# Copying V straight from its PSUM banks to the head layout, and moving the tail turns, in a recurrent-memory attention kernel

## The chip, the cores and the metric

The kernel runs on one core of one Trainium2 chip, in one launch. The metric is the device time of that core in microseconds (us), from the first to the last instruction. Most executions of one kernel agree within 0.3%, so a difference of a few us needs several rounds on the same chip.

## The reference, cut to what matters

The program computes a transformer block with a memory-augmented, recurrent attention and a gated feed-forward part, and the gradients of all weights and inputs. The change concerns the forward pass of the attention alone. There the sequence of 2048 rows is cut into 64 segments of 32 rows; each segment attends to itself and to 8 memory rows, and the first 8 rows of its result are the memory of the next. So segments can't run at the same time: the end of one is the beginning of the next.

```python
B, S, Dm = (1, 2048, 512); H, Dh = (32, 128); M, seg = (8, 32)
for s in range(n_seg):                               # 64 segments, one after the other
    xs = x[:, s * seg_len:(s + 1) * seg_len, :]
    h = jnp.concatenate([mem, xs], axis=1)           # 40 rows
    q = jnp.einsum('btd,dhe->bhte', h, Wq)
    k = jnp.einsum('btd,dhe->bhte', h, Wk)
    v = jnp.einsum('btd,dhe->bhte', h, Wv)
    scores = jnp.where(mask, jnp.einsum('bhqe,bhke->bhqk', q, k) * scale, -1e9)
    p = _softmax(scores, axis=-1)
    o = jnp.einsum('bhqk,bhke->bhqe', p, v)
    o = jnp.einsum('bhte,hed->btd', o, Wo)
    mem = o[:, :M, :]                                # the next segment's memory
    outs.append(o[:, M:, :])
```

## The kernel before

**The layouts.** A projection multiplies the 32 first rows of a segment (the memory and 24 rows of its own) by all 32 heads. TensorE does it in 128x32 tiles, so one PSUM bank of 128 partitions holds four groups of heads, 32 rows each, side by side in the partitions. Groups 0 to 2 already lie where attention wants them: the head layout packs three heads into 96 partitions. Group 3 (partitions 96 to 127) holds the last eight heads, the "far" ones, and these must move to partitions 0 to 95. The last 8 rows of each segment (the "tail" rows) don't depend on the memory; they are projected four segments at a time, ahead of need, and brought in separately.

**One segment** runs in this order. `proj` projects one half of the heads and copies the bank to rows in SBUF (`RA`). `turns` transposes the K and Q rows on TensorE; each turned bank is then copied by ScalarE or VectorE, first the "own" heads, then the far ones.

```python
def turn_half(self, psp, rows, hf):                  # one tile (one bank) per tensor and half
    tp = psp.tile([128, 4, 128], BF16, name="turn_ps", tag="p")
    for i in range(4):
        self.nc.tensor.transpose(tp[:, i, :], rows[...], self.ident[:, :])
    return tp
...
proj("k", 0, "dve"); proj("k", 1, "act")             # line breaks joined
proj("q", 0, "dve"); proj("q", 1, "act")
proj("v", 0, "dve")
nc.gpsimd.tensor_copy(Vst[0:96, 0:512], RA["v"][0:96, 0:512])
turns()
proj("v", 1, "dve")
nc.gpsimd.tensor_copy(Vst[0:96, 512:1024], RA["v"][0:96, 512:1024])
...
st_exp(0)                                            # scores on TensorE, exponential on ScalarE
st_exp(1)
vshift()                                             # the moving product
st_exp(2)
```

V needs no transpose, only its far heads moved. That is `vshift`: three TensorE products with an identity block carry partitions 96 to 127 of the V rows to partitions 0 to 95 of a PSUM bank, and VectorE copies the bank to `Vst`.

```python
def vshift():
    sh = ps_f32("sh_ps")
    shf = sh[:].rearrange("p g x -> p (g x)")
    for hl in range(3):
        nc.tensor.matmul(shf[32 * hl:32 * hl + 32, 0:384], lhsT=self.ident[96:128, 96:128],
                         rhs=RA["v"][96:128, 384 * hl:384 * hl + 384], start=True, stop=True,
                         tile_position=(96, 32 * hl))
    nc.vector.tensor_copy(Vst[0:96, 1024:1408], shf[0:96, 0:384])
```

Then come, in three parts of 4, 4 and 3 groups of heads, the denominators (`den`, products with ones), PV (`pv`), the reciprocals, the scaled results `Ost`, their turns (`ott`) and the output projection. The denominators of all groups lie in the last column block of one bank, `or2`, whose first three blocks later take the third part of PV.

```python
or2 = ps_f32("or_ps")
den(0, or2); or0 = pv(0); ...
den(1, or2); or1 = pv(1)
recip(0, 2, or2)                                     # VectorE reads or2[:, 3, 0:8]
ost(0, or0, "dve")
ost(1, or1, "act")                                   # four scalings
pv(2, or2)                                           # TensorE writes or2[:, 0:3, :]
den(2, or2); recip(2, 3, or2); ost(2, or2, "dve")
...
fill(s4, "turn")                                     # tail turns: s4 = s % 4 of 2 and 3
if s4 == 3:
    p1(s // nseg_t + P1_AHEAD, 4)                    # the turns of a later tile's layer norm
    turned = True
if more and not turned:
    mask_mm(more.pop(0))                             # the next segment's mask, put into a score bank
    mask_mm(more.pop(0))
ott(0)
... # a mask between the turns that follow, where one is left
ott(1); ott(2)
at_ps = outproj()
```

The program order of each engine is kept by dependencies that the kernel adds itself. All tiles with `tag="p"` share five PSUM buffers of one bank each; the scores have three of their own.

Of the kernel before, what the change touches and what calls it, by code (L numbers as in the profile page):

```python
# [7 lines left out]
BF16 = mybir.dt.bfloat16  # L8
# [32 lines left out]
class K:  # L41
# [392 lines left out]
    def phase2(self):  # L434
        nc, tc, cfg, io = self.nc, self.tc, self.cfg, self.io
        D, DC, H, E, L, M, T, G, NS = cfg.D, cfg.DC, cfg.H, cfg.E, cfg.L, cfg.M, cfg.T, cfg.G, cfg.NS
        GW = 128
        NP = 3
# [9 lines left out]
        with ExitStack() as ctx:  # L448
# [10 lines left out]
            def ps_f32(name):  # L459
                return psp.tile([128, PG, GW], F32, name=name, tag="p")  # L460
# [4 lines left out]
            def ptiles(name, n, zero=True, w=G * GW):  # L465
                ts = []
                for i in range(n):
                    t = pt.tile([128, w], BF16, name=f"{name}{i}")
                    if zero:
                        zeros.append(lambda t=t, w=w: nc.vector.memset(t[:, 1024:w] if w == 9 * 128 else t[:], 0.0))  # L470
                    ts.append(t)
                return ts
# [6 lines left out]
            Vsts = ptiles("Vst", 2)  # L479
            Ost = ptiles("Ost", 1)[0]  # L480
            OT = ptiles("OT", 1)[0]
            RAs = [{x: ptiles(f"RA{i}" + x, 1, w=9 * 128)[0] for x in ("vkq", "kq")[i]} for i in range(2)]
            RAs[1]["v"] = RAs[0]["v"]
            RB = {x: ptiles("RB" + x, 1, w=9 * 128)[0] for x in "kq"}
            RBv = ptiles("RBv", 2, w=9 * 128)

# [1 line left out]
            P1_AHEAD = 2  # L488
# [64 lines left out]
            def part3(t, pi):  # L553
                return t[:, pi * PW:min((pi + 1) * PW, G * GW)].rearrange("p (g x) -> p g x", x=GW)
# [7 lines left out]
            Ws = {"q": Wq, "k": Wk, "v": Wv}  # L562

            def pass_half(x, hf, lhs, rows, eng):
                self.col_pass(psp, Ws[x], hf, lhs, rows, eng)

            def turn_half(rows, hf):
                return self.turn_half(psp, rows, hf)

            def to_heads(eng, xt, src, i0, n, w, o, own=True, far=True):  # L570


                b = 0 if w == 32 else 96
                s4 = src.rearrange("p i (j r) -> p i j r", r=32)
                if own:
                    d = xt[:, 120 * i0:120 * (i0 + n)].rearrange("p (i x) -> p i x", x=120)[:, :, b:b + 3 * w]
                    self.evac(eng, d.rearrange("p i (j r) -> p i j r", r=w), s4[:, :, 0:3, o:o + w])
                if not far:
                    return
                for a0, n0, hl in ((0, 3, 0), (3, 3, 1), (6, 2, 2)):  # L580
                    lo, hi = max(a0, i0), min(a0 + n0, i0 + n)
                    if lo < hi:
                        d = xt[:, 960:1320].rearrange("p (i r) -> p i r", r=120)[:, lo - a0:hi - a0]
                        self.evac(eng, d[:, :, b + w * hl:b + w * hl + w], s4[:, lo - i0:hi - i0, 3, o:o + w])

            def rows_out(rows, dram, s0, ns):

                if ns == 1:
                    nc.sync.dma_start(dram[s0, 0:96, 0:8, :].rearrange("r g e -> r (g e)"), rows[0:96, 0:1024])
                    nc.sync.dma_start(dram[s0, 0:96, 8:11, :].rearrange("(hl r) g e -> r hl (g e)", r=32),  # L590
                                      rows[96:128, :].rearrange("r (hl x) -> r hl x", hl=3))
                    return
                for j in range(3):
                    nc.sync.dma_start(dram[s0:s0 + 4, 96 + 8 * j:104 + 8 * j, 0:8, :].rearrange("s q g e -> s q (g e)"),
                                      rows[32 * j:32 * j + 32, 0:1024])
                for hl in range(3):
                    nc.sync.dma_start(dram[s0:s0 + 4, 96 + 8 * hl:104 + 8 * hl, 8:11, :].rearrange("s q g e -> s q (g e)"),
                                      rows[96:128, 384 * hl:384 * hl + 384])
# [44 lines left out]
            def fill(s4, where):  # L643
                for f in slots.pop((s4, where), []):
                    f()
# [35 lines left out]
            for s in range(NS):  # L681
# [9 lines left out]

                def proj(x, hf, eng):
                    pass_half(x, hf, lambda c: hT[:, c, :], RA[x], eng)
                    if hf == 1 and x != "v" and s < NS - 1:
                        rows_out(RA[x], DR[x], s, 1)

                def late_rows():
                    for x in "kq":
                        rows_out(RA[x], DR[x], s, 1)

                def turns():
                    tps = []
                    for x in "kq":
                        for hf in range(2):
                            tps.append((x, hf, ("act", "dve")[hf], turn_half(RA[x], hf)))
                            to_heads(tps[-1][2], XT[x], tps[-1][3][:], 4 * hf, 4, 32, 0, far=False)
                    for x, hf, eng, tp in tps:
                        to_heads(eng, XT[x], tp[:], 4 * hf, 4, 32, 0, own=False)

                def st_exp(pi):  # L710
                    st_ps = masked.pop(pi)
# [21 lines left out]
                        nc.tensor.transpose(ps[:, j, :], src[:, g * w:g * w + GW], self.ident[:, :])  # L733
                    return ps[:, 0:n, :], n

                def vshift():
                    sh = ps_f32("sh_ps")
                    shf = sh[:].rearrange("p g x -> p (g x)")
                    for hl in range(3):
                        nc.tensor.matmul(shf[32 * hl:32 * hl + 32, 0:384], lhsT=self.ident[96:128, 96:128],  # L740
                                         rhs=RA["v"][96:128, 384 * hl:384 * hl + 384], start=True, stop=True,
                                         tile_position=(96, 32 * hl))
                    nc.vector.tensor_copy(Vst[0:96, 1024:1408], shf[0:96, 0:384])

                def pv(pi, or_ps=None):
                    or_ps = or_ps or ps_f32("or_ps")
                    n = min(PG, G - pi * PG)
# [6 lines left out]
                def ost(pi, or_ps, eng):  # L754
                    n = min(PG, G - pi * PG)
                    if eng == "act":
                        for j in range(n):
                            g = pi * PG + j
                            nc.scalar.activation(Ost[0:120, g * GW:(g + 1) * GW], or_ps[0:120, j, :], AF.Copy,
                                                 scale=rden[:, g:g + 1])  # L760
                        return
                    nc.vector.tensor_tensor(part3(Ost, pi)[0:120, 0:n, :], or_ps[0:120, 0:n, :],
                                            rden[:, pi * PG:pi * PG + n].unsqueeze(2).to_broadcast([120, n, 128]), op=ALU.mult)

                def ott(pi):
                    ps, n = transposes_part(Ost, pi)
                    self.evac("dve" if pi == 1 else "act", part3(OT, pi)[:, 0:n, :], ps)

                def outproj():
                    ps = psp.tile([128, 256], F32, name="at_ps", tag="p")  # L770
# [18 lines left out]
                if s == 0:  # L789
                    for f in firsts["q"]:  # L790
                        f()
                    tails_in("kq", 0)
                proj("v", 0, "dve")
                nc.gpsimd.tensor_copy(Vst[0:96, 0:512], RA["v"][0:96, 0:512])
                turns()
                proj("v", 1, "dve")
                nc.gpsimd.tensor_copy(Vst[0:96, 512:1024], RA["v"][0:96, 512:1024])
                if s == 0:
                    for f in firsts["v"]:
                        f()  # L800
# [7 lines left out]
                    late_rows()  # L808
                st_exp(0)
                st_exp(1)  # L810
                vshift()
                st_exp(2)
                if s < NS - 1:
                    nc.sync.dma_start(VTr[:], Vst[:, :], transpose=True)
                or2 = ps_f32("or_ps")
                den(0, or2)
                or0 = pv(0)
# [8 lines left out]
                recip(0, 2, or2)  # L826
                ost(0, or0, "dve")
                ost(1, or1, "act")
                pv(2, or2)
                den(2, or2)  # L830
                recip(2, 3, or2)
                ost(2, or2, "dve")
                more = list(range(NP)) if s + 1 < NS else []
                turned = bool(slots.get((s4, "turn"))) or bool(mod_r)
                mod_row = mod_r.pop()() if mod_r else None
                if s + 1 in mod_at:
                    load, products = self.mod_rest(psp, sb2, mod_at.index(s + 1))
                    load()
                    mod_r.append(products)
                fill(s4, "turn")  # L840
                if s4 == 3:
                    p1(s // nseg_t + P1_AHEAD, 4)
                    turned = True
                if more and not turned:
                    mask_mm(more.pop(0))
                    mask_mm(more.pop(0))
                ott(0)
                if len(more) > 1:
                    mask_mm(more.pop(0))
                ott(1)  # L850
                if len(more) > 1:
                    mask_mm(more.pop(0))
                ott(2)
                if more:
                    mask_mm(more.pop(0))
                self.pop_later()
                self.pop_later()
                nc.sync.dma_start(self.OSR[s], gl3(Ost))
# [1279 lines left out]
```

The softmax here doesn't subtract the row's maximum and nothing guards it: scores larger than these inputs give would overflow.

## Time and profile before

| | |
|---|---|
| median of 3 runs | 3096.84 us (3094.25 to 3099.61) |
| span of the profiled run | 3093.9 us |
| TensorE clock granted, mean | 0.991 of full |
| first K turn of the first and of the last segment | 46.7 and 985.2 us |
| one cycle of four segments, 601.00 to 660.52 us | 59.52 us |
| mean DMA rate over the span | 227 GB/s |

The 64 segments of the forward attention fill the time from about 47 to about 1000 us, a third of the span. The rest (layer norms, feed-forward part, all gradients) isn't touched by the change. The views read here are the page with the busy share of each engine, the windows view (busy time of each engine in given stretches), the timeline (instructions in order of time, equal neighbours merged into one line), the chain of waits inside a window, and the answers for one tile or one line, which also tell what an engine waited for. In these, PE is TensorE's products, PEld its weight loads, DVE VectorE, ACT ScalarE and POOL GpSimd; the name of a tile stands without its buffer number. A product on PE is shown with its modelled length, pipelining included, so its start is the safer reading.

### The profile page before, as it was taken

Reading aid. Unit: us, or ns where it says so; the run is one execution under the profiler, and the core shown is the slowest. Engines: PE = TensorE matmul, PEld = TensorE weight load, DVE = VectorE, ACT = ScalarE, POOL = GpSimd, SP = SyncE. Lnnn points to the kernel's source line nnn. Section 1 sums busy time; section 2 is a strip of 40 time slices with the busy share of each in tenths; the row PEclk is TensorE's granted clock in tenths of the full one; section 3 lists DMA queues with packets and bytes.
Section 4 is the critical chain, followed back from the end, with each engine's and each line's share of the span. In section 5 each row is a group of like instructions: output and inputs, shape, how many; then the busy total and the mean of one; then the engine's idle time right before and its main releaser. Section 6 shows DMA issues by size and latency. Waiting matters only on the chain.

```text
span 3093.9 us, 106049 instructions
## 1 busy us (share of the span) xinstructions
PE 2997.4 (97%) x43769; PEld 1835.7 (59%) x43845; DVE 1628.3 (53%) x3799; ACT 1269.5 (41%) x3056; POOL 1378.6 (45%) x2958
## 2 busy tenths in 40 slices
PE   5999999999999899989999999999999999999999
PEld 3666666666665444445577777777777754445454
DVE  4556656665555788742255555555555642322221
ACT  2555555555555433322255555555555530111011
POOL 3666766666766222211244444444444422333322
PEclk8999999999999899999999999999999999999999
DMA  9887788788788799997599999999999998666574
GB/s 299 217 213 203 205 206 216 201 213 211 206 201 255 200 231 232 224 284 247 170 239 243 245 243 244 239 248 244 244 240 245 245 271 279 195 201 220 190 237 148
DMA packets 845944, 703.54 MB, mean 227 GB/s; under 512 B 544306, under 2 KB 717906, under 8 KB 845076
## 3 DMA queue, kind: packets, MB, share of 16 engines
q1 hardware_dynamic: 714148, 486.69, 62.3%
q0 software_dynamic: 60656, 148.64, 14.9%
q10 hardware_dynamic: 70656, 61.41, 6.4%
q8 instruction: 345, 5.65, 0.8%
q14 instruction: 139, 1.14, 0.1%
HBM read 294.93 MB, written 276.35 MB: 185 GB/s over the span
## 4 chain that ended last, share of the span: by engine, by line
PE 90%; DMA 4%; DVE 3%; issue 1%; POOL 1%; ACT 1%; SPq 0%; another core or an unknown queue 0%; DVEq 0%; POOLq 0%; ACTq 0%
PE pass_ps L255 18%; PE gps L1928 13%; PE dh_ps L215 8%; PE g_ps L1590 6%; PE gps5o L1942 4%; PE at_ps L223 4%; PE dhq_ps L223 4%; PE gps L1277 3%; PE mm L1121 3%; PE dh_tps L215 3%; PE turn_ps L264 2%; PE dp_ps L1569 2%; PE tps L1502 2%; PE tps L733 2%; PE mm L1081 2%; DVE RA0v L63 1%
## 5 line engine op out<-in xcount | busy, mean ns | idle before, releaser
L1928 PE MATMUL gps<-rows,hrows 128*128 128x512 bf16 (+2 forms) x2124 | 415.6, 355 | 1.9
L1928 PEld LDWEIGHTS <-hrows 128*128 128x128 bf16 x2160 | 211.2, 98 | 204.6
L255 PEld LDWEIGHTS <-hT 128*32 128x32 bf16 x6144 | 158.2, 97 | 161.3 <-issue 1.9
L1634 POOL COPY dOst<-RAd 96x512 bf16<-96x512 bf16 x128 | 75.4, 612 | 312.2 <-DVE RAd L63 312.2
L63 DVE CAST ot<-gps 128x512 bf16<-128x512 f32 (+3 forms) x76 | 48.1, 633 | 274.8 <-PE gps L1928 185.8
L1932 POOL DMA_DIRECT2D out_dram<-ot x108 | 81.3, 753 | 248.9 <-DVE ot L63 136.5
L61 ACT ACTIVATE ot<-gps 128x512 bf16<-128x512 f32 (+3 forms) x75 | 41.3, 551 | 349.5 <-PE gps L1928 221.7
L885 POOL TENSOR_TENSOR Pst<-Pst,rden 120x1408 bf16<-120x1408 bf16 x63 | 159.6, 2533 | 43.8 <-issue 28.4
L61 ACT ACTIVATE dVT<-g_ps 128x512 bf16<-128x512 f32 (+1 forms) x192 | 109.5, 570 | 95.3 <-PE g_ps L1590 95.0
L63 DVE CAST RA0v<-pass_ps 128x512 bf16<-128x512 f32 x128 | 88.5, 692 | 89.4 <-PE pass_ps L255 85.5
L215 PE MATMUL dh_ps<-WvT,dVT 128*32 128x512 bf16 x2048 | 133.4, 380 | 0.2 <-DVE RBd L63 0.2
L255 PE MATMUL pass_ps<-Wv,hT 128*32 128x512 bf16 x2048 | 133.3, 380 | 0.0
L1942 PE MATMUL gps5o<-WoT,rows 128*128 128x512 bf16 x580 | 127.8, 379 | 3.9 <-DMA rows<-OSR 3.2
L255 PE MATMUL pass_ps<-Wk,hT 128*32 128x512 bf16 x2048 | 123.3, 383 | 1.5 <-ACT hT L875 1.1
L1579 DVE SCALAR_TENSOR_TENSOR dS<-dp_ps,Pst_l 128x512 bf16<-128x512 f32 (+1 forms) x192 | 112.1, 640 | 22.1 <-PE dp_ps L1577 22.1
L223 PE MATMUL at_ps<-Wo,OT 128*32 128x256 bf16 x4096 | 123.5, 273 | 0.1
L255 PE MATMUL pass_ps<-WoT,dyT 128*32 128x256 bf16 (+1 forms) x3072 | 122.4, 308 | 0.9 <-ACT dyT L1708 0.9
L223 PE MATMUL dhq_ps<-WqT,dQT 128*32 128x256 bf16 x4096 | 122.9, 273 | 0.0
L215 PE MATMUL dh_ps<-WkT,dKT 128*32 128x512 bf16 x2048 | 122.2, 380 | 0.0
L255 PE MATMUL pass_ps<-Wq,hT 128*32 128x512 bf16 x2048 | 121.6, 379 | 0.0
L223 PEld LDWEIGHTS <-dQT 128*32 128x32 bf16 x4096 | 109.6, 97 | 15.9
L717 ACT ACTIVATE ET<-st_ps 128x480 bf16<-128x480 f32 (+1 forms) x192 | 96.0, 535 | 42.6 <-ACT qT L61 34.7
(419 smaller groups left out, 7082.2 us busy)
## 6 DMA issues: line engine op xcount, KB each, us to landing
OSR<-Ost SPq DMA_DIRECT2D x64, 352.0 KB
OT<-OT SPq DMA_DIRECT2D x64, 352.0 KB
VT<-VTr SPq DMA_DIRECT2D x64, 352.0 KB
PS<-Pst SPq DMA_DIRECT2D x64, 352.0 KB
OT_l<-OT SPq DMA_DIRECT2D x64, 352.0 KB
Pst_l<-PS SPq DMA_DIRECT2D x64, 352.0 KB
VT_l<-VT SPq DMA_DIRECT2D x64, 352.0 KB
DVR<-rows_x POOLq DMA_DIRECT2D x64, 352.0 KB, 6.4
```

Source lines behind the costliest of these rows:

```text
L61: return nc.scalar.activation(out, in_, AF.Copy)
L63: return nc.vector.tensor_copy(out, in_)
L215: self.nc.tensor.matmul(ps[32 * j:32 * j + 32, :], lhsT=lhsT, rhs=w, start=(n < 4), stop=(n >= total - 4), tile_position=(0, 32 * j))
L223: nc.tensor.matmul(ps[32 * j:32 * j + 32, :], lhsT=x[k], rhs=w[k][:, 256 * d:256 * d + 256], start=(n == 0), stop=(n == total - 1), tile_p ...
L255: self.nc.tensor.matmul(ps[32 * j:32 * j + 32, :], lhsT=lhs(c), rhs=rhs, start=(c == 0), stop=(c == DC - 1), tile_position=(0, 32 * j))
L717: nc.scalar.activation(part3(ET, pi)[:, 0:n, 0:120], st_ps[:, 0:n, 0:120], AF.Exp, scale=cfg.scale)
L885: nc.gpsimd.tensor_tensor(Pst[0:120, :, :], Pst[0:120, :, :], rden[:, :].unsqueeze(2).to_broadcast([120, G, 128]), op=ALU.mult)
L1121: nc.tensor.matmul(hp[:], lhsT=xT[:, fc, :], rhs=wT[:, fc, :], start=(n == 0), stop=(n == 2 * FC - 1))
L1579: nc.vector.scalar_tensor_tensor(out=part3(dS, pi), in0=ps[:, 0:n, :], scalar=cfg.scale, in1=part3(Pst, pi), op0=ALU.mult, op1=ALU.mult)
L1590: nc.tensor.matmul(ps[:, j, :], lhsT=lh[:, g * GW:(g + 1) * GW], rhs=rh[:, g * GW:(g + 1) * GW], start=True, stop=True)
L1928: nc.tensor.matmul(ps[:, 0:ng * E], lhsT=hrows[:, tp_, c * 128:(c + 1) * 128], rhs=rows[:, tp_, 0:ng * E], start=(tp_ == 0), stop=(tp_ == ...
L1942: nc.tensor.matmul(pss[gg][:], lhsT=src[0][:, src[1], gg * E:(gg + 1) * E], rhs=dyrows[:, tp_, :], start=(tp_ == order[0]), stop=(tp_ == o ...
```

## The change

V goes from its two banks straight to `Vst`: VectorE copies the own heads of each half, and the far heads are copied across partitions by ScalarE (first half) and VectorE (second half). The moving products, the V rows in SBUF and GpSimd's two copies of them are gone. The V banks now stay in use until the far copies have read them; the turns of K and Q, which took four tiles, take two, so that K's and Q's turns of one half share a tile. Tail turns, modulation products and (where s mod 4 = 3) the layer norm's turns move ahead to where TensorE waits for the exponentials and reciprocals. Mask products stand one before each turn of `Ost`, and the engines that copy the turned results are chosen anew. The aim is to take work off TensorE and to fill its waits. The diff, cut to its core:

```diff
-            RAs = [{x: ptiles(f"RA{i}" + x, 1, w=9 * 128)[0] for x in ("vkq", "kq")[i]} for i in range(2)]
-            RAs[1]["v"] = RAs[0]["v"]
+            RAs = [{x: ptiles(f"RA{i}" + x, 1, w=9 * 128)[0] for x in "kq"} for i in range(2)]
...
+                def proj_v(hf):
+                    ps = pass_half("v", hf, lambda c: hT[:, c, :], None, None)
+                    self.evac("dve", Vst[0:96, 512 * hf:512 * hf + 512], ps[0:96, :])
+
+                    def far(eng):
+                        for hl in range(3):
+                            lo, hi = max(384 * hl, 512 * hf), min(384 * hl + 384, 512 * hf + 512)
+                            if lo < hi:
+                                self.evac(eng, Vst[32 * hl:32 * hl + 32, 1024 + lo - 384 * hl:1024 + hi - 384 * hl],
+                                          ps[96:128, lo - 512 * hf:hi - 512 * hf])
+
+                    return far
...
                 def turns():
-                    tps = []
-                    for x in "kq":
-                        for hf in range(2):
-                            tps.append((x, hf, ("act", "dve")[hf], turn_half(RA[x], hf)))
-                            to_heads(tps[-1][2], XT[x], tps[-1][3][:], 4 * hf, 4, 32, 0, far=False)
-                    for x, hf, eng, tp in tps:
-                        to_heads(eng, XT[x], tp[:], 4 * hf, 4, 32, 0, own=False)
+                    tps = [psp.tile([128, 8, 128], BF16, name="turn_ps", tag="p") for _ in range(2)]
+                    for k, x in enumerate("kq"):
+                        for hf, eng in enumerate(("act", "dve")):
+                            tp = tps[hf][:, 4 * k:4 * k + 4, :]
+                            for i in range(4):
+                                nc.tensor.transpose(tp[:, i, :], RA[x][:, (4 * hf + i) * 128:(4 * hf + i + 1) * 128],
+                                                    self.ident[:, :])
+                            to_heads(eng, XT[x], tp, 4 * hf, 4, 32, 0, far=False)
+                    for k, x in enumerate("kq"):
+                        for hf, eng in enumerate(("act", "dve")):
+                            to_heads(eng, XT[x], tps[hf][:, 4 * k:4 * k + 4, :], 4 * hf, 4, 32, 0, own=False)
...
-                def vshift():                        # the whole function, shown above
...
-                    self.evac("dve" if pi == 1 else "act", part3(OT, pi)[:, 0:n, :], ps)
+                    self.evac(eng, part3(OT, pi)[:, 0:n, :], ps)
...
-                proj("v", 0, "dve")
-                nc.gpsimd.tensor_copy(Vst[0:96, 0:512], RA["v"][0:96, 0:512])
+                far = proj_v(0)
                 turns()
-                proj("v", 1, "dve")
-                nc.gpsimd.tensor_copy(Vst[0:96, 512:1024], RA["v"][0:96, 512:1024])
+                far("act")
+                far = proj_v(1)
+                far("dve")
...
                 st_exp(1)
-                vshift()
                 st_exp(2)
...
+                more = list(range(NP)) if s + 1 < NS else []
+                mod_row = mod_r.pop()() if mod_r else None   # modulation products, s4 = 0
...
+                fill(s4, "turn")
                 or2 = ps_f32("or_ps")
                 den(0, or2)
                 or0 = pv(0)
...
                 ost(1, or1, "act")
+                if s4 == 3:
+                    p1(s // nseg_t + P1_AHEAD, 4)
                 pv(2, or2)
...
                 ost(2, or2, "dve")
...   # their old places, and the two masks ahead of ott(0), are gone
+                if more:
+                    mask_mm(more.pop(0))
+                ott(0, "dve")
+                if more:
+                    mask_mm(more.pop(0))
+                ott(1, "act")
+                if more:
+                    mask_mm(more.pop(0))
+                ott(2, "dve")
```

More of the change, by code (lines that the diff above doesn't have):

```diff
@@ L564, in pass_half @@
             def pass_half(x, hf, lhs, rows, eng):
-                self.col_pass(psp, Ws[x], hf, lhs, rows, eng)
-            def turn_half(rows, hf):
-                return self.turn_half(psp, rows, hf)
+                return self.col_pass(psp, Ws[x], hf, lhs, rows, eng)
             def to_heads(eng, xt, src, i0, n, w, o, own=True, far=True):
@@ L693, in proj @@
                     pass_half(x, hf, lambda c: hT[:, c, :], RA[x], eng)
-                    if hf == 1 and x != "v" and s < NS - 1:
+                    if hf == 1 and s < NS - 1:
                         rows_out(RA[x], DR[x], s, 1)
+                def proj_v(hf):
[8 more added lines that the diff above has]
+                    return far
                 def late_rows():
@@ L734, in transposes_part @@
                     return ps[:, 0:n, :], n
-                def vshift():
[L737 to L743, printed above, removed]
                 def pv(pi, or_ps=None):
@@ L763, in ost, with ott @@
                                             rden[:, pi * PG:pi * PG + n].unsqueeze(2).to_broadcast([120, n, 128]), op=ALU.mult)
-                def ott(pi):
+                def ott(pi, eng):
                     ps, n = transposes_part(Ost, pi)
-                    self.evac("dve" if pi == 1 else "act", part3(OT, pi)[:, 0:n, :], ps)
+                    self.evac(eng, part3(OT, pi)[:, 0:n, :], ps)
                 def outproj():
@@ L814, in phase2 @@
                     nc.sync.dma_start(VTr[:], Vst[:, :], transpose=True)
+                more = list(range(NP)) if s + 1 < NS else []
+                mod_row = mod_r.pop()() if mod_r else None
+                if s + 1 in mod_at:
+                    load, products = self.mod_rest(psp, sb2, mod_at.index(s + 1))
+                    load()
+                    mod_r.append(products)
+                fill(s4, "turn")
                 or2 = ps_f32("or_ps")
@@ L832, in phase2 @@
                 ost(2, or2, "dve")
[L833 to L853, printed above, removed]
                 if more:
                     mask_mm(more.pop(0))
+                ott(0, "dve")
[5 more added lines that the diff above has]
+                ott(2, "dve")
                 self.pop_later()
```

## The prediction

> **What bounds the kernel now.** I read the page first: TensorE is busy almost without a break, in the forward pass (slices 1 to 13) as elsewhere, at full clock.
>
> ```profile
> PE 2997.4 (97%) x43769; PEld 1835.7 (59%) x43845; DVE 1628.3 (53%) x3799; ACT 1269.5 (41%) x3056; POOL 1378.6 (45%) x2958
> PE   5999999999999899989999999999999999999999
> PEclk8999999999999899999999999999999999999999
> ```
>
> But a busy TensorE can still be waiting, since the ends of its matmuls are modelled. So I took one cycle of four segments (the windows view: span; busy time and count of each engine; clock; DMA share; GB/s). It holds, in order, a segment with nothing to turn for the tails (s mod 4 = 1), two that turn tail K and tail Q (2, 3), and one with the modulation products (0).
>
> ```profile
> 601.00:615.59 14.59, 14.44 (x272) 8.80 (x268) 9.16 (x24) 7.45 (x20) 11.13 (x24) 1.00 0.72 181
> 615.59:630.56 14.97, 14.81 (x279) 9.21 (x275) 8.97 (x23) 7.88 (x21) 10.03 (x22) 1.00 0.89 217
> 630.56:645.49 14.93, 14.80 (x285) 9.37 (x280) 8.22 (x22) 8.32 (x22) 9.61 (x21) 1.00 0.93 241
> 645.49:660.52 15.03, 14.90 (x287) 9.53 (x283) 9.10 (x25) 7.65 (x21) 10.31 (x22) 1.00 0.65 191
> ```
>
> No other engine fills a segment; what counts is TensorE's order and the places where it waits. The chain of waits inside the first of these segments (start, length, what) shows them:
>
> ```profile
> 604.13 0.70 DVE RA0v L63
> 604.84 0.04 issue
> 604.88 0.34 PE sh_ps L740 x2
> ...
> 605.92 0.22 DVE rden L726
> 606.13 0.04 issue
> 606.18 0.33 PE or_ps L750 x3
> ```
>
> The chain leaves TensorE twice. The moving products (sh_ps) wait for VectorE's copy of the second half of V; and the third PV group (or_ps x3) waits for a reciprocal. The line of the moving products says the same of all segments ("issue", us and times):
>
> ```profile
> L740 PE MATMUL sh_ps<-RA0v,ident x192: 317/332/332, 50.9 to 988.1; 32*32 32x384 bf16 x192
>   issue: 20.3, 63
> ```
>
> That is 0.32 us of weight-load idle per segment (20.3/63). The whole stop is longer: first moving product at 604.47, next scores at 605.15, so 0.68 us, or 43 us over 64 segments. This is what the change seems to offer.
>
> **What the skill says.** (1) "PSUM — Partial Sum Buffer", section "PSUM bank collisions raise a hardware error": two engines on one bank in one quadrant collide even at disjoint columns, and reads collide with reads; software must keep them apart. The trace shows that this kernel's dependencies do it. The third PV group writes columns 0 to 2 of a bank whose column 3 holds the denominators that the reciprocal reads; nothing in the data links them, yet it starts at 606.18, 0.05 us after the reciprocal's end (605.92 + 0.21). Over all 64 segments that gap is 0.054 us in the median, and never under 0.053. Reads are kept apart too: VectorE's half of a turned tail tile waits for ScalarE's half. From the answer for turn_ps (idle until, us and times):
>
> ```profile
>   ACT b_colsq L61: 11.3, 16
>   ACT b_colsk L61: 10.4, 16
> ```
>
> (2) "TensorEngine Tiling (Array Packing)", "Key Properties": changing the tiling mode drains TensorE. Here a turn follows a turn by 0.056 us, but the V pass (128x32 tiles) follows the last turn by 0.149, so about 0.09 a change. The moving products are two more changes of mode, part of the 0.68. (3) "ScalarE: Activation LUTs", "What ACT_TABLE_LOAD costs": 186 ns + 0.833 per column, neighbours overlapping by about 93 ns. As an estimate, the far copies of 384 and 128 columns take 0.51 and 0.29 us, less the overlap. The trace's copy of 384 columns from PSUM took 0.490, which agrees.
>
> **The change part by part.** All times below are us after T, the first K turn of a segment (601.97 in the shown one). The turns before:
>
> ```profile
> 602.43 0.61 PE L264 MATMUL turn_ps<-ident,RA1q 128*128 128x128 bf16 x8
> 602.46 0.49 ACT L61 ACTIVATE kT<-turn_ps 128x384 bf16<-128x384 bf16 x1 [0.64 <-PE turn_ps L264]
> 602.97 0.40 PE L255 MATMUL pass_ps<-Wv,hT 128*32 128x512 bf16 x4
> ```
>
> *Moved: the turns share banks.* Four tiles become two; K's and Q's turns of one half lie in one bank. Q's turns start at 0.46 today while ScalarE begins to read K at 0.49. After the change they write the bank that ScalarE reads, so by (1) they wait for it: its copy ends at 0.98, plus 0.05 is 1.04. The eight Q turns take 0.22 + 0.22 (VectorE's K copy ends at 1.14, in time for the second four), so the last starts at 1.43, and the second V half starts 0.149 later at **1.58 instead of 1.00**. Everything behind moves by 0.58: that half takes 0.98 to the scores, which start at S = 2.56 instead of 1.98.
>
> *Removed: the moving products.* 0.68 us leaves TensorE's order between second and third scores. But the exponentials set the next step: the first starts 0.47 after S (604.41 - 603.95), they follow each other by 0.467, and one takes 0.57. So they start at 3.03 and 3.49, and the second ends at 4.06. The denominators of part 1 need that: 4.12. Today they start at 3.67 (605.64), only 0.13 after their earliest time (exponential's end 605.45 plus 0.06). **Of the 0.68 us, 0.13 is on the path;** the rest turns into waiting for ScalarE.
>
> *Added: far copies.* Two on ScalarE (0.51, 0.29), queued behind its last Q copy, which ends at 2.48: they occupy ScalarE to about 3.09, with the overlap just in time for the exponential at 3.03. Two on VectorE of 256 columns: casts of 512 and 384 columns take 0.692 and 0.554, so 256 take about 0.42. They follow the second V cast (2.75 to 3.44) and end at 4.1, before the reciprocal at 4.40. The VectorE cast of sh_ps (0.55) and two GpSimd copies of 0.61 go. None is on the path.
>
> *Moved: tail turns and modulation products* (0.49 and about 0.55) go between scores and denominators. There they fill TensorE from 3.14 to about 3.65, when the first exponential is ready: hidden. They leave the place before the Ost turns, and one mask product (0.20) stays there.
>
> *The rest of the path.* Reciprocal 4.40 to 4.61 (4.15 today, +0.45). VectorE's first Ost 0.73 after that, 5.34; Ost turns from 5.39; a mask to 5.82; second turns, held to 5.98 by ScalarE's four Ost scalings, which end 1.31 after the reciprocal; done at 6.04; mask to 6.20; third turns to 6.36. Then the row turns (0.056 each, two where s mod 4 = 1; in 0 also the tail sum, 0.20) and a mode change of 0.09. The output projection starts at 6.72, 6.57, 6.51, 6.51 for s mod 4 = 0, 1, 2, 3. The first OT copy, moved to VectorE, is ready at 6.37 and holds nothing.
>
> Today's medians of the same distance, from the start times in the trace, are 6.61, 6.16, 6.27, 6.50. Differences +0.11, +0.41, +0.24, +0.01: **+0.77 us in four segments, 16 times is +12 us.** That sum already contains the gain, the mask moved to better places and the OT copy (today the projection waits for it on ScalarE where s mod 4 = 1). Behind the projection nothing changes. 3096.8 + 12 is 3109; I take 3107, as a few waits may overlap more than I can see.
>
> **Rivals.** *(a) No wait at the shared bank*, if the dependencies follow columns. Then S stays, the moving products and idle places go, and each segment gains about 0.58 - 0.19 = 0.39 us: 25 us less, 3072. Against it are both bank waits above. 5%. *(b) TensorE's work sets the time*, each moving product removed being saved: 43 us, 3054. Against it: the exponential ends only 0.13 before it limits. 2%. *(c) ScalarE becomes the bound*: if far copies take 0.2 longer than the estimate, every exponential and all behind it slips, 64 x 0.2 = 13 us more, 3120. The slack is about nil, so this is the likeliest error upwards. *(d) PSUM buffers*: the tail tile now lives through PV, with five buffers shared; a late buffer before the Ost turns could add 0.1 to 0.3 us in three segments of four, 5 to 15 us. Against it: the second V tile is free by 4.2, in time.
>
> **Range and chances.** The mechanism gives +12; an error of 0.25 us per segment in either direction is 16 us. So 3086 to 3126, with (a) and (b) below it. A 2% change is 62 us or 0.97 us in every segment, more than any of these alone: faster 0.02, within 2% 0.95, slower 0.03.
>
> **What would show it.** The Q turns start about 1.04 after the first K turn, not 0.46, right behind ScalarE's K copy. The scores run without a break. TensorE idles before the denominators where s mod 4 = 1, and hardly elsewhere. The reciprocal comes 0.45 later after T. If the Q turns start at 0.46, the first step is wrong and (a) holds. If exponentials start well after S + 0.47, (c) holds.

## The result, and the profile after

The changed kernel takes **3143.95 us** (median of 4 runs, 3142.95 to 3145.13) against 3096.63 us: the ratio is 1.0152, with an interval of 1.0135 to 1.0170. The prediction said 3107, with a range up to 3126: the direction was right, but the loss is 47 us and not 10.

The page of the changed kernel, the lines that answer to those of before (busy time and share of each engine; TensorE's busy tenths; its clock):

```profile
PE 2988.8 (95%) x43653; PEld 1829.9 (58%) x43653; DVE 1661.4 (53%) x3926; ACT 1287.2 (41%) x3120; POOL 1304.9 (42%) x2830
PE   5999999999999799989989999999999999999999
PEclk8999999999999899999999999999999999999999
```

TensorE has less to do (2988.8 for 2997.4 us) and the clock is the same; what grew is its idle time. The windows view of one cycle of four segments (s mod 4 = 1, 2, 3, 0; columns as before) says where:

```profile
627.48:642.82 15.34, 14.07 (x269) 8.69 (x265) 9.74 (x25) 7.71 (x21) 9.02 (x20) 1.00 0.73 159
642.82:658.10 15.28, 14.46 (x276) 9.10 (x272) 9.48 (x24) 8.20 (x22) 9.24 (x22) 1.00 0.78 213
658.10:673.53 15.43, 14.73 (x280) 9.23 (x276) 8.71 (x23) 8.69 (x23) 8.39 (x19) 1.00 0.81 234
673.53:689.33 15.80, 14.83 (x284) 9.47 (x280) 9.61 (x26) 7.86 (x22) 9.71 (x23) 1.00 0.63 194
```

The stretches are 0.3 to 0.8 us longer, and in the first, TensorE is busy for 14.07 us of 15.34, where it was 14.44 of 14.59. Over all segments the medians of a segment's length went from 15.04, 14.59, 14.70 and 14.93 us (s mod 4 = 0, 1, 2, 3) to 15.80, 15.34, 15.28 and 15.43: 2.59 us in four, 16 times is 41 us. The forward pass as a whole ends 43.8 us later. Of the rest, 4 us lie between feed-forward part and attention gradients, a stretch that took 184 to 192 us in the profiles of this study, without a change to it; I don't count them.

The chain of waits inside the first of these segments (start, length, what) holds three of the causes:

```profile
628.07 0.50 ACT kT L61
628.57 0.04 issue
628.62 0.61 PE turn_ps L716 x8
...
629.82 0.23 ACT qT L61 x2
630.05 0.03 issue
630.07 0.48 ACT Vst L61
630.56 0.01 issue
630.57 0.28 ACT Vst L61
630.85 0.01 issue
630.87 0.58 ACT ET L730
...
632.25 0.02 DVEq L739
632.27 0.04 issue
632.31 0.22 DVE rden L739
```

The moving products are gone. In their place stand, first, ScalarE's copy of K, which holds back the eight Q turns; then ScalarE's two far copies of V (ACT Vst), each beginning only when the one before has ended, and behind them the exponential (ACT ET); last, a semaphore step (DVEq) ahead of the reciprocal that wasn't there before. Today's line of the Q turns in the timeline ends with its wait in brackets (idle before, and who ended it):

```profile
628.62 0.61 PE L716 MATMUL turn_ps<-ident,RA1q 128*128 128x128 bf16 x8 [0.42 <-ACT kT L61]
```

The table puts the main steps in us after the first K turn, T (at 627.58 in this segment). The start times are medians over the segments; the first two and the reciprocal's end are the same in all four kinds of segment.

| step | before | predicted | after |
|---|---|---|---|
| first scores | 1.98 | 2.56 | 2.55 |
| first exponential | 2.45 | 3.03 | 3.29 |
| end of the first reciprocal | 4.16 | 4.61 | 4.94 |
| first Ost turn | 4.94 to 5.12 | 5.39 | 5.72 |
| output projection, s mod 4 = 0 | 6.61 | 6.72 | 7.37 |
| 1 | 6.16 | 6.57 | 6.91 |
| 2 | 6.27 | 6.51 | 6.85 |
| 3 | 6.50 | 6.51 | 7.00 |

The scores come where they were predicted; what was missed lies behind them.

### The profile page after: what moved, and what is told of

Its sections match the earlier page's. It is cut to its first block, busy times and chain, and to the rows that moved or that the text cites. A ratio compares the mean times of both kernels' runs of the same rounds, so it can differ in the third digit from the quotient of the medians.

```text
span 3141.1 us, 105861 instructions
## 1 busy us (share of the span) xinstructions
PE 2988.8 (95%) x43653; PEld 1829.9 (58%) x43653; DVE 1661.4 (53%) x3926; ACT 1287.2 (41%) x3120; POOL 1304.9 (42%) x2830
## 4 chain that ended last, share of the span: by engine, by line
PE 84%; DMA 5%; ACT 5%; DVE 3%; issue 2%; POOL 1%; SPq 1%; ACTq 0%; DVEq 0%; POOLq 0%
PE pass_ps L255 16%; PE gps L1926 13%; PE dh_ps L215 8%; PE g_ps L1588 6%; PE gps5o L1940 4%; PE at_ps L223 4%; PE dhq_ps L223 4%; PE gps L1275 3%; PE mm L1119 3%; PE dh_tps L215 3%; PE dp_ps L1567 2%; PE turn_ps L716 2%; PE tps L1500 2%; PE mm L1079 2%; PE tps L746 1%
## 5 line engine op out<-in xcount | busy, mean ns | idle before, releaser
L63 DVE CAST Vst<-pass_ps 96x512 bf16<-96x512 f32 (+1 forms) x256 | 142.6, 557 | 83.7 <-PE pass_ps L255 79.8
L338 POOL DMA_DIRECT2D AOA<-at_rb x64 | 36.1, 564 | 217.6 <-DVE at_rb L334 210.1
```

The costliest lines, as they stand in the source:

```text
L63: return nc.vector.tensor_copy(out, in_)
```

## The experiments

My theory after the result: the loss is a sum of waits, with the shared turn bank the largest (0.57 us a segment, 37 us), the queue on ScalarE in front of the exponential next (0.26, 17 us), then the reciprocal's semaphore and late PSUM buffers. The rivals: that the tail turns' new place is to blame; that the sharing of banks is bad in any order; that the removal of the moving products was worth 43 us and something much larger ate it. Unless another is named, ratios are against the kernel before the change. Differences in us against the change are between medians of different rounds, and the kernel before moved by up to 2 us between those. So I add what the segments alone gained in the profiled run, measured from the first K turn of the first segment to that of the last: 938.5 us before the change and 981.2 after it, a loss of 42.7.

### Four turn banks: four_banks

```diff
-                    tps = [psp.tile([128, 8, 128], BF16, name="turn_ps", tag="p") for _ in range(2)]
...
+                            tp = tps[x, hf] = psp.tile([128, 4, 128], BF16, name="turn_ps", tag="p")
```

> The changed kernel with one part undone: the turns of K and Q in four banks again. If the shared bank costs what the first scores show (they come 2.55 us after the first K turn, 1.98 before the change), the scores return to 1.98 and every segment gains 0.57 us: 64 x 0.57 = 37 us, so about 3107 us. The exponential should still start 0.73 us after the scores, as ScalarE's queue is as long. Rival: the scores come earlier but the exponentials, late for another reason, stay where they are: gain under 10 us.

Measured: 3132.68 us, ratio 1.0110 (1.0095 to 1.0126), so 11 us better than the change (8 in the segments) and not 37. The Q turns do follow at once, but now the second half of V waits. TensorE's timeline (first K turn at 622.08):

```profile
622.54 0.61 PE L716 MATMUL turn_ps<-ident,RA1q 128*128 128x128 bf16 x8
623.80 0.40 PE L255 MATMUL pass_ps<-Wv,hT 128*32 128x512 bf16 x4 [0.65 <-ACT kT L61]
```

The wait ends when ScalarE has read the far K heads, that is, when the first turn bank comes free. All five buffers were full: four turn banks, and the first V bank, which the change keeps until ScalarE's far copies. So the scores come at 2.69, even later than with shared banks. The gain comes from ScalarE, which has emptied its queue by then: the exponential starts 0.47 after the scores. My expectation overlooked that the longer life of the V bank and the shared turn banks belong together.

### The turns before the copies: turn_order

```diff
-                    for k, x in enumerate("kq"):
-                        for hf, eng in enumerate(("act", "dve")):
-                            ...                      # four turns, then the copy of the own heads
+                    for hf in range(2):
+                        for k, x in enumerate("kq"):
+                            ...                      # all sixteen turns
+                    for far in (False, True):
+                        ...                          # then all copies, in the old order
```

> The two shared banks stay, only the order changes: all turns first (K and Q of the first half, then of the second), and the copies after them. If it is the write into a bank that another engine still reads that costs, TensorE has no wait left in the turns, the scores come at 1.98, and instead ScalarE's K copy starts about 0.22 later than with four banks (0.71 after the first K turn, not 0.49). Its queue then ends about 2.85 and the exponential starts at 2.87, against 3.29 in the changed kernel: 0.42 us a segment, 27 us, about 3117. Rival: sharing a bank is bad in itself, in any order: no gain.

Measured: 3113.18 us, ratio 1.0053 (1.0038 to 1.0068): 31 us better than the change (26 in the segments). The timeline (first K turn at 611.10) shows TensorE without a wait and ScalarE's K copy a little later:

```profile
611.78 0.39 PE L715 MATMUL turn_ps<-ident,RA1q 128*128 128x128 bf16 x4
611.82 0.49 ACT L61 ACTIVATE kT<-turn_ps 128x384 bf16<-128x384 bf16 x1 [0.86 <-PE turn_ps L715]
612.10 0.40 PE L255 MATMUL pass_ps<-Wv,hT 128*32 128x512 bf16 x4
```

The scores are back at 1.98, the K copy starts 0.72 after the first turn, and the denominators come at 3.50 for 3.91, the 0.42 expected. So the bank wait is shown by itself, with the same two banks and the same instructions: it is not the sharing that costs, but a turn that is written into a bank between two reads of it. It is the largest single part of the loss.

### ScalarE without its far copies: no_far_act

```diff
                 turns()
-                far("act")
                 far = proj_v(1)
```

> The changed kernel without ScalarE's two far copies; the far heads of the first half of V are left out, so part of PV is computed on zeros. If these copies are what delays the exponential (it starts 0.73 us after the scores, 0.47 before the change), it returns to 0.47, and each segment gains 0.26 us: 17 us, about 3127. Rival: the exponential is late for another reason (a semaphore, the bank): no gain.

Measured: 3127.58 us, ratio 1.0096 (1.0080 to 1.0111), with the far heads of the first half left out: 16 us better than the change, in the segments too. The scores stay at 2.55 and the first denominators move from 3.91 to 3.65 in the segments with s mod 4 = 1, 2 and 3 (to 3.79 in 0, where the modulation products are in front of them). The copies delay the exponential by 0.27 (it starts at 3.02 without them, at 3.29 with them), as the theory says.

### The same copies without the jump between partitions: far_same_quadrant

```diff
-                far("act")
+                self.evac("act", junk[0:32, 0:384], far_ps[0:32, 0:384])
+                self.evac("act", junk[0:32, 384:512], far_ps[0:32, 384:512])
```

> The same two ScalarE copies in size, but read from partitions 0 to 31 and written to partitions 0 to 31 of a spare tile (the far heads of the first half are left out of PV). If the delay comes from the jump between groups of 32 partitions, which keeps ScalarE from starting an instruction before the one before has ended, the copies overlap with their neighbours by about 0.09 us each and the exponential starts at about 0.48 to 0.55 after the scores: gain 0.18 to 0.25 us a segment, 12 to 16 us, about 3130. If only the length of the copies counts, nothing changes: 3144.

Measured: 3125.24 us, ratio 1.0089 (1.0072 to 1.0105): the whole cost of the far copies is gone (16 us in the segments, as in no_far_act), although both copies are done. ScalarE's timeline (first K turn at 632.50):

```profile
634.61 0.36 ACT L61 ACTIVATE qT<-turn_ps 128x96 bf16<-128x96 bf16 x2
634.82 0.63 ACT L61 ACTIVATE junk<-pass_ps 32x384 bf16<-32x384 f32 x2
635.52 1.03 ACT L733 ACTIVATE ET<-st_ps 128x480 bf16<-128x480 f32 x2
```

The first copy starts at 634.82, while the Q copies still run until 634.97; the two take 0.63 us together, where the chain of the changed kernel has 0.48 and 0.28 with a gap; and the exponential starts at 3.02, 0.47 after the scores, as before the change. In the changed kernel each of these three joints waited for the end of the instruction before. In the median the first far copy began 0.025 us after the end of the last Q copy (here 0.151 before it), and the second 0.012 after the end of the first (here 0.102 before it).

The joints also tell which side counts. The far copies read from partition 96 and write to 0 and 32; the Q copy before them reads from and writes to 0. So at the first joint only the input's start changes, at the second only the output's, and each lost the overlap: either side alone is enough here, as far as these joints show it; no run moved one side alone. The third joint, to the exponential, changes both.

### A third buffer for the reciprocals: rden_three

```diff
-                rden = sb2.tile([120, G], F32, name="rden")
+                rden = sb2.tile([120, G], F32, name="rden", bufs=3)
```

> The changed kernel with three buffers for the reciprocals in place of two. In the changed kernel the reciprocal waits for a second semaphore, GpSimd's, and starts 0.36 us after the first denominator product of part 1, against 0.28 before the change, where VectorE had already met that semaphore when it overwrote the V rows that GpSimd copied. With a third buffer the wait is for an older use, which VectorE has met in the copy of the turned results: 0.08 us a segment, 5 us, about 3139. Rival: the 0.08 has another cause, no gain.

Measured: 3138.75 us (3137.83 to 3143.65), ratio 1.0133 (1.0118 to 1.0148). By time alone, 5 us is near the edge of what the runs separate; the trace is plainer: the first Ost turn moves from 5.72 to 5.65 in all four kinds of segment, 0.07 each, and the semaphore step ahead of the reciprocal is gone from the chain (first K turn at 622.88):

```profile
627.29 0.23 PE or_ps L734 x4
627.52 0.02 issue
627.54 0.22 DVE rden L739
```

### The tail turns put back: tail_back

```diff
-                fill(s4, "turn")                     # with the modulation products, ahead of den(0)
...
                 ost(2, or2, "dve")
+                fill(s4, "turn")                     # here again; the layer norm's turns too
```

> The changed kernel with the tail turns, the modulation products and the layer norm's turns put back behind the denominators of part 2, ahead of the Ost turns. If their new place hides them in the wait for the exponentials, putting them back costs, beyond the 0.3 us for which TensorE waits for VectorE's Ost there: 0.2 us where s mod 4 = 2, 0.4 in 3, 0.3 in 0, none in 1: 0.9 x 16 = 14 us, about 3158. Rival: the move of the tail turns is what made the kernel slower; then this is faster than 3144.

Measured: 3155.95 us, ratio 1.0188 (1.0173 to 1.0203), 12 us worse than the change (10 in the segments). The Ost turns start at 6.07, 5.72, 5.88 and 6.11 for s mod 4 = 0, 1, 2, 3, where the change has 5.72 in all. So moving the tail turns is right, and the rival that blames it falls.

### Before the change, without the moving products: no_shift

```diff
                 st_exp(1)
-                vshift()
                 st_exp(2)
```

> The kernel before the change with its moving products and VectorE's copy of their bank left out, nothing in their place (the far heads of V stay zero in PV). This is the whole gain that the removal can bring. If the exponentials set the next step, the denominators of part 1 move only from 3.67 to 3.54 us after the first K turn: 0.13 us a segment, 8 us, about 3090. Rival: TensorE's order sets the time, all of 0.68 us comes back: 43 us, about 3055.

Measured: 3089.89 us, ratio 0.9977 (0.9968 to 0.9986), with the far heads of V left out: 8 us (8 in the segments too), not 43. TensorE's timeline:

```profile
599.72 0.75 PE L715 MATMUL st_ps<-qT,kT 128*128 128x120 bf16 x11
600.82 0.25 PE L721 MATMUL or_ps<-ones,ET 128*128 128x1 bf16 x4 [0.34 <-ACT ET L717]
```

All eleven scores run in one piece, and then TensorE waits for the exponential. The stop of 0.68 us that looks like the prize in the profile of before was four fifths hidden.

### Other engines for the turned results: ott_engines

```diff
-                ott(1, "act")
+                ott(1, "dve")
...
-                ott(2, "dve")
+                ott(2, "act")
```

> The changed kernel with VectorE copying the second turned part and ScalarE the third (the change has it the other way round). Where s mod 4 = 0 the projection starts at 7.37 us after the first K turn, 0.05 after ScalarE's copy of the second part, though the last turn is done at 6.96: it seems to wait for that buffer. VectorE would have it free at about 7.07, so 0.25 us in these segments and nothing in the others: 4 us, about 3140. Rival: it waits for something else and nothing changes.

Measured: 3139.59 us, ratio 1.0136 (1.0122 to 1.0150). The projection of s mod 4 = 0 starts at 7.06 for 7.37, the other three are unchanged. In the timeline of the changed kernel (first K turn at 611.78, s mod 4 = 0) the wait is written at the projection itself:

```profile
618.50 0.60 ACT L61 ACTIVATE OT<-tps 128x512 bf16<-128x512 bf16 x1 [0.46 <-PE tps L746]
619.15 0.40 PE L223 MATMUL at_ps<-Wo,OT 128*32 128x256 bf16 x8 [0.24 <-ACT OT L61]
```

That copy holds the second part of the results, which the projection needs only 0.66 us after its start; and where s mod 4 = 1 it starts at 6.91 with the same copy running until 7.32; so what it waits for is the copy's PSUM buffer. That explains 0.31 us in one segment of four.

### What follows: far_first, far_split and far_first_two

```diff
 # on top of turn_order, rden_three and ott_engines
+                v_far(v0_ps, 0, 0, "act")            # 384 columns, before the turns
+                v_far(v0_ps, 0, 1, "act")            # 128; far_first_two: "dve", behind the turns
+                v_own(v0_ps, 0)                      # VectorE
                 turns()
+                v1_ps = v_pass(1)
+                v_own(v1_ps, 1)
+                v_far(v1_ps, 1, 1, "dve")
...
                 st_exp(2)
+                v_far(v1_ps, 1, 2, "act")
```

> A version that follows from the runs so far: all turns before the copies (as in turn_order); ScalarE copies the two far pieces of the first half of V before the turns, in time that it has idle, and VectorE its own heads after that; of the second half one far piece goes to VectorE, the other to ScalarE after the exponentials; three reciprocal buffers; VectorE copies the second turned part, ScalarE the third, so that the buffer the projection waits for where s mod 4 = 0 comes free earlier. If ScalarE's queue ahead of the exponential is what is left to win, it starts 0.47 after the scores, the reciprocal ends at about 4.03 after the first K turn (4.15 before the change) and the projection starts 0.16, 0.33, 0.41 and 0.40 us earlier than before the change in the four segments: 21 us, about 3077. Rival: VectorE's own copies, now late, delay the scores of part 1, and half of it is lost: 3088 or more.

> As far_first, but the first half's far pieces split: 128 columns on VectorE behind its own copy, before the turns are ready, 384 columns on ScalarE behind the turns. ScalarE's queue then ends at 2.6 after the first K turn, so the exponential starts 0.62 after the scores, 0.15 later than in far_first: about 10 us more, 3087. Rival: VectorE's earlier copies matter more, and it is the faster of the two.

> far_first with the smaller of ScalarE's two early far pieces (128 columns) given to VectorE, behind its copies of K and Q. VectorE's copy of its own V heads then starts at about 0.62 us after the first K turn, not 0.92, and the last far K and Q copies end at about 2.36, not 2.53, so that the third scores need not wait (they come at 2.68 in far_first, 0.27 after the second). Where TensorE has something to fill in, the denominators come up to 0.2 us earlier: in all 0.4 us in four segments, 6 us, about 3081. Rival: VectorE's queue behind it gets too long and the reciprocal slips: 3087 or more.

Measured: far_first 3087.35 us, ratio 0.9964 (0.9951 to 0.9977); far_split 3094.31, ratio 0.9988 (0.9981 to 0.9994); far_first_two 3085.59, ratio 0.9960 (0.9947 to 0.9972). All three beat both kernels, and all three less than I expected. In far_first the segments with s mod 4 = 1 go as drawn (Ost turns at 4.81), but VectorE's late copies hold back the third scores, and the tail turns and modulation products behind them: the Ost turns are at 5.08, 4.87 and 4.96 in 0, 2 and 3. far_first_two mends that: the third scores join the others, and the denominators come at 3.07 in three of the four kinds. Its ScalarE and TensorE (first K turn at 592.57):

```profile
592.68 0.48 ACT L61 ACTIVATE Vst<-pass_ps 32x384 bf16<-32x384 f32 x1 [0.27 <-PE pass_ps L255]
594.54 0.75 PE L726 MATMUL st_ps<-qT,kT 128*128 128x120 bf16 x11
595.01 1.40 ACT L728 ACTIVATE ET<-st_ps 128x480 bf16<-128x480 f32 x3 [0.39 <-ACT qT L61]
```

The far copy lies in time that ScalarE had idle, and the exponential is free again, 0.47 after the scores. In the segments the single runs gained 26 us (turn_order), 16 (no_far_act), 5 (rden_three) and 5 (ott_engines) against the change, 52 together; far_first gained 55. Set against the loss of 42.7, the 52 leave about 10 us of gain, near the 8 that no_shift measured for the moving products. So the four waits account for the loss, though not to the last us: far_first moves the far copies, where no_far_act left them out.

## Why the prediction was right in kind and wrong in size

- **What bounds the segment: right.** The prediction put 0.13 us of the moving products' 0.68 on the path, 8 us in all; no_shift measured 8 us. The reading that did it was the end of the exponential set beside the start of the denominators.
- **The shared banks: right.** "Everything behind moves by 0.58": the scores came at 2.55 for 2.56, and turn_order shows that the wait is ScalarE's read of the bank, as the Trainium skill's page "PSUM — Partial Sum Buffer", section "PSUM bank collisions raise a hardware error", requires of software. Rival (a) falls: the Q turns start at 1.04 and not at 0.46.
- **The far copies: the step that failed.** "They occupy ScalarE to about 3.09, with the overlap just in time for the exponential at 3.03." Their lengths were right (0.485 and 0.272 us in the trace, for 0.51 and 0.29), but I counted on the overlap of 0.09 at each joint although the start partition changes there. No joint overlapped, three times in a row, and the exponential came at 3.29 in the median, 0.26 late: 17 us over 64 segments. The Trainium skill's page "VectorE: DVE Perf Modes", section "Two Vector instructions with no wait between them", says for VectorE that an instruction whose start quadrant (group of 32 partitions) changes waits for those before. The trace agrees: VectorE's two far copies began 0.032 and 0.013 us after the end of the one before, where its far K and Q copies overlap by 0.083. far_same_quadrant shows the like on ScalarE. Rival (c) had named the danger ("the slack is about nil") at 13 us; I gave its cost, but left it out of the sum.
- **The reciprocal: a term that was missing.** It starts 0.36 us after the denominators and not 0.28. The prediction listed GpSimd's two copies as removed and "None is on the path". But with them went VectorE's only early wait on GpSimd, so the reciprocal has to wait for GpSimd by an extra semaphore step (DVEq in the chain): 0.07 to 0.08 us, 5 us. With rden_three's third buffer the step is gone.
- **The buffers: rival (d) was in part right.** It expected 0.1 to 0.3 us in three segments of four; it is 0.31 where s mod 4 = 0, at the projection and not before the Ost turns, and about 0.15 in 3, where the second Ost turns start 0.05 after ScalarE's last scaling. This second one had no run of its own.
- **The tail turns: right.** They are hidden in the wait for the exponentials, and tail_back measured 12 us for them (10 in the segments).

In sum, the missed terms are 4 x 0.26, 4 x 0.07, 0.31 and 0.15 us, 1.78 in four segments; the difference between predicted and measured starts of the projection is 0.65 + 0.34 + 0.34 + 0.49 = 1.82. Sixteen times that is 29 us; with the 12 of the prediction it makes the 41 by which the segments grew. The range was argued from an error of 0.25 us per segment, 16 us, and reached 19 us above the number; the mean error was 0.46. That was too little for a path on which ScalarE had no slack: each error there is multiplied by 64.

## What to carry to other kernels

Ask of each removed wait what ends next: the time between the start of what waits and the end of what it needs tells how much of a visible stop is on the path, here 0.13 of 0.68 us. When tiles of several engines are packed into one PSUM bank, write the bank completely before the first reader is issued; the same banks and instructions in another order were 26 us faster over the segments. And when a copy goes to an engine that stands in front of the critical step, look for the idle time earlier in its queue rather than for a free engine.

## What the runs showed of the hardware that I had not expected

In these traces ScalarE overlaps neighbouring copies by 0.10 to 0.15 us only as long as they start at the same partitions, on the input side and on the output side. Two copies of 384 and 128 columns, 32 partitions high, took 0.77 us from partition 96 to partitions 0 and 32, beginning after the end of the copy before; the same two took 0.63 us from partition 0 to partition 0 and began 0.15 us before the end of the copy before. With the joint to the exponential the jump cost 0.27 us in the median segment.
